# Experts' token lists built in SBUF by one-hot products, with DRAM lists only for experts over 384 tokens

## The chip, the cores and the metric

The kernel runs on one core of a Trainium2 chip. The metric is the device time of one execution in microseconds; less is better. Engines are named as in the profile: PE (TensorE matmuls) and PEld (its weight loads), DVE (VectorE), ACT (ScalarE), POOL (GpSimd) and SP (SyncE, which here only issues DMAs).

## What is computed

Block-sparse attention, and a mixture of experts with one expert for a token and a skip score, on its result. In the reference, cut to what matters:

```python
# attention: q, k, v are 4 x 8 x 768 x 64, blocks of 32, 24 blocks
mask = window | first or last block of the row or of the column | 3 sampled blocks for each query block
attn = softmax(where(mask, q @ k.T / 8, -1e9));  x = (attn @ v), as 3072 rows of 512
# experts: 8 of them, 512 -> 1024 -> 512
do_compute = x @ w_skip > 0
logits = x @ w_gate;  e = argmax(logits);  gate = softmax(logits)[e]
out = x;  out[do_compute] += gate * (relu(x @ w1[e]) @ w2[e])
```

Which tokens an expert gets is known only once attention has made `x`. So the kernel keeps, for each expert, a list of its tokens' numbers with their gates, and uses it to gather rows of `x` and to scatter the results back into `out`.

## The kernel before, in words

**Attention.** The work is a list of units: 16 dense ones (first and last query block, all keys) and then 88 sparse ones, four for each of the query blocks (tiles) 1 to 22, one for each batch. A loop over `k` (lines 645 to 704) writes out by hand what each engine gets: in step `k` come the scores `S` of unit `k + 3` (L400 in sparse units), the sums `N` of unit `k - 1`, the copy `V` and the product `A` of unit `k` (L434), the exponentials `X` of `k + 2`, the turning `T` of `k + 1` (L420) and the maxima `M` of `k + 3` (L408, L409). With the fourth unit of a tile, POOL gets the copies of the keys of the tile after next (`load_k`, L186 and L201), SP the loads of its queries and values (L208 to L220), and after `A` the stores of the finished rows to `out` (L455). In each step `fetch` (L629) adds at most two small routing steps, taken from the lists `urgent` and `todo`: their PE part behind the unit's PE work, their DVE part before or behind `M`, their POOL part at the end.

**Routing.** Tiles are routed in seven batches (`BATCHES`, L38: four of four tiles, two of three, one of two; batch 0 includes the dense tiles). `route` (L223) gives seven steps for a batch: logits on PE (`p0`, L238), their turning (`p1`, L247), three DVE steps with an exponential on ACT, the rank of each token among its expert's (`rank`, L257 to L260, which reads `cum`, the counts so far), its slot (`d3`, L280), and the address of its list entry (`d4`, L287 to L292). At the end of `d4` POOL issues one indirect DMA for each tile of the batch (L302, shown as L72, where the helper `scatter_to` stands): 128 entries of 8 bytes, token and gate, go to the DRAM tensor `lst`. All PE results of routing steps share one PSUM tile, `rps`, with a single buffer.

`lst` holds for each of 128 partitions 8 x 26 entries (`E * LC`): entry `c` of partition `p` is the token number `128 c + p` of the expert. It is first filled with "no token" by a DMA from ACT's queue (L138 to L141).

**Hand-over.** Near the end of attention `pick_first` (L510) takes the fullest expert so far as first one; `look_first` (L534) counts again, reads the first two chunks of that expert's list (`le`, L547, POOL's queue), gathers these 256 rows of `out` into `xe` (L551 to L553) and turns them for PE (`rows`, L555 to L564). The line with `timed` (L644) sets the steps of `k` at which its five parts enter `urgent`. From unit 94 on, SP loads the first weights (L488), and POOL makes the low part of the first one (L494).

In `If(pv > 1)` (L978 to L1016) the first expert's matrix product runs on these early rows while the seventh batch (tiles 21 and 22, `last`) is routed between its eight blocks: `beside` (L983) lists what goes between. Then `counts` and `lists` (L836, L847) read the token counts and the whole list back into SBUF (`lt`, through SP's queue), `order_lists` (L850) puts the first expert in front, and POOL gathers further rows (`rows`, L856). The queue of SP holds behind that read the second half of a weight (`load_w("2", 1, 1, 2)`) and the next weights. PE turns the third chunk of the first expert (L1002, shown as L588) between two parts of the second product.

**The other experts.** A loop over seven experts (L1034 to L1036) with branches on the count of tokens (`gemm1_any`, `outputs`) covers up to 384 tokens (three chunks, `CS`) of each. Whoever has more is treated behind it, in `If(top > CG * CS)` (L1040 to L1059), which is not entered with these inputs: no row of the profile has one of its lines.

Of the kernel before, what the change touches and what calls it, by code (L numbers as in the profile page):

```python
# [41 lines left out]
def tile_kernel(ctx, tc, qs, qd, kt, v, sb, wg, w1, w2, out):  # L42
# [3 lines left out]
    dram = ctx.enter_context(tc.tile_pool(name="dram", bufs=1, space=DRAM))  # L46

    lst = dram.tile([P * E * LC, 2], I32, name="lst")
# [174 lines left out]
    def route(xta, tiles):  # L223

        T = len(tiles)
        st = {}
        lgv = lambda: st["lg"][:, :, 0:E]
# [25 lines left out]
        def rank():  # L253
# [20 lines left out]
            lambda: V.tensor_copy(out=small("pay", [P, T, 2], I32, 2)[:, :, 0], in_=tokens),  # L274
# [8 lines left out]
            lambda: V.reciprocal(out=st["pay"].bitcast(F32)[:, :, 1], in_=st["es"]),  # L283
# [8 lines left out]
            lambda: V.scalar_tensor_tensor(out=small("adr", None, I32, 2), in0=st["lo"], scalar=float(E * LC), in1=st["hi"], op0=ALU.mult, op1=ALU.add),  # L292
# [95 lines left out]
    class Sparse:  # L388
# [61 lines left out]
        def after(self):  # L450
# [19 lines left out]
            if i == tiles[-1]:  # L470
                todo.extend(lambda n=n: route_step(g, tiles, n) for n in range(7))
# [61 lines left out]

    def look_first():  # L534
# [4 lines left out]
        le = rt.tile([P, 2, 2], I32, name="le")  # L539
        early["l"] = le  # L540
# [4 lines left out]
        def fetch_list():  # L545
            er = nc.gpsimd.value_load(perm[0:1, 0:1], min_val=0, max_val=E - 1)
            nc.gpsimd.dma_start(out=le, in_=lst.rearrange("(p c) w -> p c w", p=P)[:, bass.ds(er * LC, 2), :])  # L547

        def fetch_rows():
            early["x"] = [rt.tile([P, DM], F32, name="xe", bufs=2) for z in range(2)]  # L550
            for z in range(2):  # L551
                nc.gpsimd.memset(early["x"][z], 0.0)
            early["g"] = [gather(early["x"][z], le[:, z, 0:1]) for z in range(2)]  # L553
# [17 lines left out]
        ], fetch_list), (None, [], fetch_rows),  # L571
# [72 lines left out]
    timed = {nu - 22 + n: (pick_first, n) for n in range(3)} | {nu - z: (look_first, n) for n, z in enumerate((12, 11, 9, 5, 4))}  # L644
# [75 lines left out]
    lt = mc.tile([P, E * LC, 2], I32, name="lt")  # L720
    ends = mc.tile([P, CS, 2], I32, name="ends")
    lsw = mc.tile([P, LC, 2], I32, name="lsw")
# [111 lines left out]
    lst3 = lst.rearrange("(p c) w -> p c w", p=P)  # L834

# [11 lines left out]
    def lists():  # L847
        nc.sync.dma_start(out=lt, in_=lst3)

    def order_lists():  # L850
        er = nc.vector.value_load(perm[0:1, 0:1], min_val=0, max_val=E - 1)
        nc.vector.tensor_copy(out=lsw, in_=lt[:, bass.ds(er * LC, LC), :])
        nc.vector.tensor_copy(out=lt[:, bass.ds(er * LC, LC), :], in_=lt[:, 0:LC, :])
        nc.vector.tensor_copy(out=lt[:, 0:LC, :], in_=lsw)

    def rows(p, cr):  # L856
        for c in cr:
            gather(xs[p % 2][c], lt[:, p * LC + c, 0:1])
# [12 lines left out]
    def close(p, c, z, xg, m=P):  # L871
        a = p * LC + c
        finish(z, xg, ltf[:, a, 1:2], lt[:, a, 0:1], m)

    def halves(p, c, y):

        wh, wl = wview("2", p)
        cs, a = slice(P * c, P * c + P), p * LC + c
# [89 lines left out]

    wt.update({"2" + t: wp2.tile([P, 4096], F32R, name=f"w2{t}") for t in "hl"})
# [8 lines left out]
    with tc.If(pv > 1) as ahead:  # L978
        px, p0, p1, d1, d2, rank, d3, d4 = last[0]()
        le = early["l"]  # L980
# [18 lines left out]
        finish(0, early["x"][0], le.bitcast(F32)[:, 0, 1:2], le[:, 0, 0:1])  # L999
# [4 lines left out]
        finish(1, early["x"][1], le.bitcast(F32)[:, 1, 1:2], le[:, 1, 0:1])  # L1004
# [26 lines left out]
    for z in range(2):  # L1031
        nc.vector.tensor_scalar(out=ends[:, :, z], in0=lt[:, (E - 1) * LC:(E - 1) * LC + CS, 0], scalar1=2.0, scalar2=float(z), op0=ALU.mult, op1=ALU.add)
# [7 lines left out]
    with tc.If(top > CG * CS):  # L1040
        for e in range(E):
            a = e * LC
            n = tokens_of(e)
            with tc.If(n > CG * CS):
# [4 lines left out]
                with tc.For_i(CS, (n + (CG - 1)) // CG, 2) as c:  # L1049
                    cur = mp.tile([P, 2, 2], I32, name="cur", bufs=1)  # L1050
                    nc.vector.tensor_copy(out=cur, in_=lt[:, bass.ds(c + a, 2), :])
# [55 lines left out]
```

## Time and profile before

| | us |
|---|---|
| runs: 601.20, 601.09, 596.47; median | 601.09 |
| profiled execution, own time | 606.04 |
| its span | 604.3 |
| PE busy in it | 513.6 |
| POOL busy in it | 216.6 |

The profile is of one execution, whose time is 4.95 us above the median of the runs. Its span leaves out 1.7 us around it. In the answers below a row of a timeline has the start, the time and the engine, then line, operation, what it writes and reads with the shapes, and how many instructions are merged; in brackets stands how long the engine had been idle and what ended that. "issue" means that the engine waited for nothing that the profile shows. L72 is the helper of all scatters, so its tiles (`lst`, or `out`) tell which one it is.

### The profile page before, as it was taken

Reading aid. Unit: us, or ns where it says so; the run is one execution under the profiler, and the core shown is the slowest. Engines: PE = TensorE matmul, PEld = TensorE weight load, DVE = VectorE, ACT = ScalarE, POOL = GpSimd, SP = SyncE. Lnnn points to the kernel's source line nnn. Section 1 sums busy time; section 2 is a strip of 40 time slices with the busy share of each in tenths; the row PEclk is TensorE's granted clock in tenths of the full one; section 3 lists DMA queues with packets and bytes.
Section 4 is the critical chain, followed back from the end, with each engine's and each line's share of the span. In section 5 each row is a group of like instructions: output and inputs, shape, how many; then the busy total and the mean of one; then the engine's idle time right before and its main releaser. Section 6 shows DMA issues by size and latency. Waiting matters only on the chain.

```text
span 604.3 us, 16232 instructions
## 1 busy us (share of the span) xinstructions
PE 513.6 (85%) x5842; PEld 382.3 (63%) x5842; DVE 369.8 (61%) x1019; ACT 251.8 (42%) x576; POOL 216.6 (36%) x236
## 2 busy tenths in 40 slices
PE   7999999899898899996979768896887958859991
PEld 4777665466565465563668558694776946737981
DVE  4877578478577777787776066544466572735510
ACT  3444455355364355462733055343153535423500
POOL 2016363564655355646372321300404040602011
PEclk9999999799899699897988898987899888979997
DMA  9999899688799499788894415441625454630000
GB/s 295 342 299 236 190 259 243 153 219 211 174 215 232 115 227 224 167 229 214 247 322 142 172 27 179 172 180 24 218 108 178 152 189 158 214 125 26 19 33 22
DMA packets 49507, 108.03 MB, mean 179 GB/s; under 512 B 7175, under 2 KB 35208, under 8 KB 43842
## 3 DMA queue, kind: packets, MB, share of 16 engines
q1 hardware_dynamic: 43760, 84.69, 51.3%
q0 software_dynamic: 5008, 20.69, 9.7%
q8 instruction: 88, 1.44, 1.0%
q14 instruction: 73, 0.60, 0.3%
q10 hardware_dynamic: 578, 0.61, 0.3%
HBM read 96.34 MB, written 12.30 MB: 180 GB/s over the span
## 4 chain that ended last, share of the span: by engine, by line
PE 34%; issue 28%; DMA 21%; DVE 8%; POOL 3%; SPq 2%; POOLq 1%; ACT 0%; ACTq 0%; DVEq 0%
PE sp L400 11%; PE op L434 7%; PE tp L420 6%; DMA kts<-w 5%; DMA out<-o,lt 5%; DMA x<-out,lt 4%; DMA lst<-pay,adr 4%; PE op L356 4%; PE sp L321 3%; DVE m L409 3%; DVE m L408 3%; PE tp L344 2%; DMA out<-xs 2%; POOL out L72 1%; DVE xs L447 1%
## 5 line engine op out<-in xcount | busy, mean ns | idle before, releaser
L400 PE MATMUL sp<-kg,q 128*64 128x256 f32 x704 | 102.0, 408 | 2.8 <-issue 2.7
L424 ACT COPY pt<-tp 128x512 f32<-128x512 f32 x88 | 51.7, 588 | 108.1 <-PE tp L420 96.7
L408 DVE TENSOR_REDUCE m<-sp 128x2 f32<-128x512 f32 x88 | 60.2, 684 | 43.3 <-PE sp L400 35.5
L72 POOL DMA_INDIRECT out<-o,lt x17 | 19.4, 1139 | 179.2 <-DVE o L829 178.9
L201 POOL TENSOR_TENSOR kg<-kts,onesf 128x512 f32<-128x512 f32 x66 | 82.0, 1273 | 0.0
L415 ACT ACTIVATE pr<-sp,m 128x256 f32<-128x256 f32 x176 | 74.4, 478 | 8.0 <-DVE rs L445 8.0
L746 PE MATMUL hp<-xh,w1h 128*128 128x256 f32 (+3 forms) x192 | 61.3, 319 | 16.7 <-issue 8.3
L186 POOL TENSOR_SCALAR kg<-kts 128x512 f32<-128x512 f32 x50 | 30.1, 627 | 125.5 <-PE sp L400 87.4
L400 PEld LDWEIGHTS sp<-kg,q 128*64 128x64 f32 x704 | 45.2, 141 | 36.5 <-issue 24.5
L420 PE MATMUL tp<-ident,pr 128*128 128x128 f32 x352 | 61.8, 297 | 4.4 <-issue 4.4
L434 PEld LDWEIGHTS op<-va,pt 128*32 128x32 f32 x1376 | 31.9, 112 | 47.3 <-ACT pt L424 24.9
L747 PE MATMUL hp<-xl,w1h 128*128 128x256 f32 (+3 forms) x192 | 60.6, 316 | 0.0
L748 PE MATMUL hp<-xh,w1l 128*128 128x256 f32 (+3 forms) x192 | 60.5, 315 | 0.0
L751 ACT ACTIVATE hh<-hp 128x256 fp32r<-128x256 f32 (+2 forms) x56 | 21.2, 381 | 93.6 <-PE hp L748 51.6
L434 PE MATMUL op<-va,pt 128*32 128x65 f32 x1376 | 49.5, 232 | 11.3 <-DVE xs L447 8.5
L434 PE MATMUL op<-vb,pt 128*32 128x65 f32 x1376 | 50.6, 227 | 3.1 <-issue 2.9
L754 DVE SCALAR_TENSOR_TENSOR hl<-hp,hh 128x256 fp32r<-128x256 f32 (+2 forms) x56 | 23.4, 419 | 46.8 <-ACT hf L753 28.4
L746 PEld LDWEIGHTS hp<-xh,w1h 128*128 128x128 f32 x192 | 39.1, 204 | 19.1 <-issue 19.1
L420 PEld LDWEIGHTS tp<-ident,pr 128*128 128x128 f32 x352 | 38.9, 145 | 14.2 <-issue 6.9
L812 PE MATMUL yp<-w2h,hh 128*128 128x512 f32 x112 | 45.0, 402 | 2.7 <-ACT w1h L492 1.6
L813 PE MATMUL yp<-w2l,hh 128*128 128x512 f32 x112 | 44.1, 394 | 0.3 <-DVE o L829 0.3
L814 PE MATMUL yp<-w2h,hl 128*128 128x512 f32 x112 | 44.2, 394 | 0.0
(207 smaller groups left out, 1013.2 us busy)
## 6 DMA issues: line engine op xcount, KB each, us to landing
vb<-v SPq DMA_DIRECT2D x68, 260.0 KB
va<-v SPq DMA_DIRECT2D x48, 260.0 KB
kts<-w SPq DMA_DIRECT2D x6, 2048.0 KB
kts<-w POOLq DMA_DIRECT2D x6, 2048.0 KB
q<-qs SPq DMA_DIRECT2D x22, 512.0 KB
vt<-v SPq DMA_DIRECT2D x16, 390.0 KB
kts<-w SPq DMA_DIRECT2D x12, 512.0 KB
kts<-kt SPq DMA_DIRECT2D x15, 384.0 KB
```

Of the source, the lines that this page charges most:

```text
L201: nc.gpsimd.tensor_tensor(out=kg[x][:, :, c0:c0 + BS], in0=kts[:, :, bass.ds(kr * BS, BS)], in1=onesf[:, 0:BS].unsqueeze(1).broadcast_to([ ...
L400: nc.tensor.matmul(out=self.sp[64 * j:64 * j + 64, g, :], lhsT=qt[self.i][:, p, :], rhs=kg[self.x][:, p, :], start=True, stop=True)
L408: lambda: nc.vector.reduce_max(out=self.mx, in_=self.sp, axis=AX.X),
L415: nc.scalar.activation(out=self.pr[:, g, :], in_=self.sp[:, g, :], func=AF.Exp, bias=self.mx[:, g:g + 1], scale=SCALE)
L420: nc.tensor.transpose(out=self.tp[:, u, :], in_=self.pr[:, u // 2, (u % 2) * P:(u % 2) * P + P], identity=ident)
L424: nc.scalar.copy(out=self.pt, in_=self.tp)
L434: nc.tensor.matmul(out=self.op[32 * hh:32 * hh + 32, g, :], lhsT=self.pt[:, 2 * g + t, 32 * hh:32 * hh + 32], rhs=vt[:, 8 * self.b + 4 * g ...
L746: nc.tensor.matmul(out=hp[:, 0:w], lhsT=wh[:, f, k, :], rhs=xh[:, k, 0:w], start=(k == 0), stop=False)
L747: nc.tensor.matmul(out=hp[:, 0:w], lhsT=wh[:, f, k, :], rhs=xl[:, k, 0:w], start=False, stop=False)
L748: nc.tensor.matmul(out=hp[:, 0:w], lhsT=wl[:, f, k, :], rhs=xh[:, k, 0:w], start=False, stop=(k == NK1 - 1))
L812: nc.tensor.matmul(out=yp, lhsT=hh[:, f, cs], rhs=wh[:, f, :], start=(f == 0), stop=False)
L814: nc.tensor.matmul(out=yp, lhsT=hl[:, f, cs], rhs=wh[:, f, :], start=False, stop=(f == NK2 - 1))
```

## The change

The lists are kept in SBUF as floating-point numbers, `lsf`, for each of 128 partitions two words (token number minus 3072, and gate) of 8 x 3 entries. An entry is put into its place by a product: for each tile POOL makes a 128x128 matrix `lo` that has a one where the slot's low seven bits say, and two 128x24 matrices `hi` that have the token's word in the column of its expert and chunk. PE multiplies them and adds the tiles of a batch up, and DVE adds the result to `lsf`. So a batch takes nine routing steps: `d4` ends with `place` on POOL instead of the scatter, then come `put` on PE and `d5` on DVE. The sum into `cum` moves from `d4` to `d5`. Two parts of `look_first` come three, and three come two units later; `le` is copied out of `lsf` by DVE. In `beside`, `put` and then `d5`, `counts` and `lists` stand one and two places later than `counts` stood. Lists read in SBUF have a stride of three chunks instead of 26 per expert. The DRAM list is made only in the last branch, for experts over 384 tokens, from the rows, columns and words that are kept for all tiles.

```diff
-    lst = dram.tile([P * E * LC, 2], I32, name="lst")
...
-    fill = kg[0].bitcast(I32).rearrange("p a c -> p (a c)")[:, 0:2 * E * LC].rearrange("p (c w) -> p c w", w=2)
-    nc.gpsimd.memset(fill[:, :, 0], N)
-    nc.gpsimd.memset(fill[:, :, 1], 0)
-    nc.scalar.dma_start(out=lst.rearrange("(p c) w -> p c w", p=P), in_=fill)
+    posi = kg[0].bitcast(I32)[:, 0, 0:P]
+    nc.gpsimd.iota(posi, pattern=[[1, P]], base=0, channel_multiplier=0)
+    pos = const.tile([P, P], F32, name="pos")
+    nc.gpsimd.tensor_copy(out=pos, in_=posi)
+    colsi = kg[0].bitcast(I32)[:, 1, 0:E * CS].rearrange("p (e c) -> p e c", e=E)
+    nc.gpsimd.iota(colsi, pattern=[[LC, E], [1, CS]], base=0, channel_multiplier=0)
+    cols = const.tile([P, E * CS], F32, name="cols")
+    nc.gpsimd.tensor_copy(out=cols, in_=colsi.rearrange("p e c -> p (e c)"))
+    lsf = const.tile([P, 2, E * CS], F32, name="lsf")
...
+    nc.gpsimd.memset(lsf, 0.0)
...
-            lambda: V.tensor_tensor(out=cum, in0=cum, in1=st["ohs"], op=ALU.add),
...
-            lambda: V.scalar_tensor_tensor(out=small("adr", None, I32, 2), in0=st["lo"], scalar=float(E * LC), in1=st["hi"], op0=ALU.mult, op1=ALU.add),
+            lambda: V.tensor_copy(out=lof, in_=st["lo"]),
+            lambda: V.tensor_copy(out=hif, in_=st["hi"]),
...
-        def scatter():
+        def place():
+            lo = st["plo"] = rt.tile([P, T * P], F32, name="lsb").rearrange("p (t x) -> p t x", t=T)
+            hi = small("phi", [P, T, 2, E * CS])
             for t in range(T):
-                scatter_to(
-                    out=lst[:, :], out_offset=bass.IndirectOffsetOnAxis(ap=st["adr"][:, t:t + 1], axis=0),
-                    in_=st["pay"][:, t, :], in_offset=None, bounds_check=P * E * LC - 1, oob_is_err=False)
+                nc.gpsimd.tensor_scalar(out=lo[:, t], in0=pos, scalar1=lof[:, t:t + 1], scalar2=1.0, op0=ALU.is_equal, op1=ALU.mult)
+                for w in range(2):
+                    nc.gpsimd.tensor_scalar(out=hi[:, t, w], in0=cols, scalar1=hif[:, t:t + 1], scalar2=pay[:, t, w:w + 1],
+                                            op0=ALU.is_equal, op1=ALU.mult)
+        def put():
+            st["lp"] = ps_r.tile([P, 2, E * CS], F32, name="rps")
+            for t in range(T):
+                nc.tensor.matmul(out=st["lp"], lhsT=st["plo"][:, t], rhs=st["phi"][:, t], start=(t == 0), stop=(t == T - 1))
+        d5 = [
+            lambda: V.tensor_tensor(out=lsf, in0=lsf, in1=st["lp"], op=ALU.add),
+            lambda: V.tensor_tensor(out=cum, in0=cum, in1=st["ohs"], op=ALU.add),
+        ]
-        return [(p0, [], None), (p1, [], None), (None, d1, None), (None, [exp] + d2, None), (rank, [], None), (None, d3, None), (None, d4, scatter)]
+        return [(p0, [], None), (p1, [], None), (None, d1, None), (None, [exp] + d2, None), (rank, [], None), (None, d3, None), (None, d4, place),
+                (put, [], None), (None, d5, None)]
...
         def fetch_list():
-            er = nc.gpsimd.value_load(perm[0:1, 0:1], min_val=0, max_val=E - 1)
-            nc.gpsimd.dma_start(out=le, in_=lst.rearrange("(p c) w -> p c w", p=P)[:, bass.ds(er * LC, 2), :])
+            er = V.value_load(perm[0:1, 0:1], min_val=0, max_val=E - 1)
+            V.tensor_copy(out=lef, in_=lsf[:, :, bass.ds(er * CS, 2)])
...
-    timed = {...} | {nu - z: (look_first, n) for n, z in enumerate((12, 11, 9, 5, 4))}
+    timed = {...} | {nu - z: (look_first, n) for n, z in enumerate((9, 8, 7, 3, 2))}
...
     def lists():
-        nc.sync.dma_start(out=lt, in_=lst3)
+        take(lt[:, :, 0], ltf[:, :, 1], lsf)
...
-        beside = [[px], [], [p0], [p1, d1], [d2], [], [], [rank, d3], [], [d4], [], [counts, lists, lambda: load_w("2", 1, 1, 2)]]
+        beside = [[px], [], [p0], [p1, d1], [d2], [], [], [rank, d3], [], [d4], [], [], [put], [d5, counts, lists, lambda: load_w("2", 1, 1, 2)]]
```

`take` is two DVE instructions that make whole numbers of the tokens and copy the gates.

More of the change, by code (lines that the diff above doesn't have):

```diff
@@ L226, in route @@
         st = {}
+        z0 = sum(len(l) for l in BATCHES[:BATCHES.index(tiles)])
+        lof, hif, pay = rows_of[:, z0:z0 + T], cols_of[:, z0:z0 + T], pays[:, z0:z0 + T]
         lgv = lambda: st["lg"][:, :, 0:E]
@@ L273, in route @@
             lambda: V.reduce_max(out=small("pm"), in_=st["pri"], axis=AX.X),
-            lambda: V.tensor_copy(out=small("pay", [P, T, 2], I32, 2)[:, :, 0], in_=tokens),
+            lambda: V.tensor_single_scalar(out=pay[:, :, 0], in_=tokens, scalar=-float(N), op=ALU.add),
             lambda: V.tensor_tensor(out=st["pri"], in0=st["pri"], in1=bc(st["pm"]), op=ALU.is_equal),
@@ L282, in route @@
             lambda: V.tensor_tensor(out=st["sl"], in0=st["sl"], in1=st["oh"], op=ALU.mult),
-            lambda: V.reciprocal(out=st["pay"].bitcast(F32)[:, :, 1], in_=st["es"]),
+            lambda: V.reciprocal(out=pay[:, :, 1], in_=st["es"]),
             lambda: V.reduce_sum(out=small("slot"), in_=st["sl"], axis=AX.X),
@@ L470, in after @@
             if i == tiles[-1]:
-                todo.extend(lambda n=n: route_step(g, tiles, n) for n in range(7))
+                todo.extend(lambda n=n: route_step(g, tiles, n) for n in range(9))
     last = []
@@ L532, in tile_kernel, with take @@
     early = {}
+    def take(ids, gates, lists):
+        nc.vector.tensor_scalar(out=ids, in0=lists[:, 0], scalar1=N + 0.25, scalar2=0.0, op0=ALU.add, op1=ALU.add)
+        nc.vector.tensor_copy(out=gates, in_=lists[:, 1])
     def look_first():
@@ L538, in look_first @@
         key, pm = (rt.tile([1, n], F32, name=m) for m, n in (("key", E), ("pm1", 1)))
-        le = rt.tile([P, 2, 2], I32, name="le")
-        early["l"] = le
+        le = rt.tile([P, 2], I32, name="le")
+        leg = rt.tile([P, 2], F32, name="leg")
+        lef = rt.tile([P, 2, 2], F32, name="lef")
+        early["l"] = le, leg
         def pe():
@@ L552, in fetch_rows @@
                 nc.gpsimd.memset(early["x"][z], 0.0)
-            early["g"] = [gather(early["x"][z], le[:, z, 0:1]) for z in range(2)]
+            early["g"] = [gather(early["x"][z], le[:, z:z + 1]) for z in range(2)]
         def rows(c):
@@ L643, in tile_kernel @@
     nu = len(units)
-    timed = {nu - 22 + n: (pick_first, n) for n in range(3)} | {nu - z: (look_first, n) for n, z in enumerate((12, 11, 9, 5, 4))}
+    timed = {nu - 22 + n: (pick_first, n) for n in range(3)} | {nu - z: (look_first, n) for n, z in enumerate((9, 8, 7, 3, 2))}
     for k in range(-LA, nu + 1):
@@ L998, in tile_kernel @@
         rows(1, range(CS))
[L999 removed]
+        finish(0, early["x"][0], leg[:, 0:1], le[:, 0:1])
         clear()
@@ L1040, in tile_kernel @@
     with tc.If(top > CG * CS):
+        lst = dram.tile([P * E * LC, 2], I32, name="lst")
+        lst3 = lst.rearrange("(p c) w -> p c w", p=P)
+        room = hf.bitcast(I32).rearrange("p a b -> p (a b)")
+        ltx, swx = (room[:, a * 2 * LC:(a + n) * 2 * LC].rearrange("p (c w) -> p c w", w=2) for a, n in ((0, E), (E, 1)))
+        adr = room[:, (E + 1) * 2 * LC:(E + 1) * 2 * LC + NC]
+        ent = mc.tile([P, NC, 2], I32, name="ent")
+        nc.gpsimd.memset(ltx[:, :, 0], N)
+        nc.gpsimd.memset(ltx[:, :, 1], 0)
+        nc.sync.dma_start(out=lst3, in_=ltx)
+        nc.vector.scalar_tensor_tensor(out=adr, in0=rows_of, scalar=float(E * LC), in1=cols_of, op0=ALU.mult, op1=ALU.add)
+        nc.vector.tensor_single_scalar(out=ent[:, :, 0], in_=pays[:, :, 0], scalar=float(N), op=ALU.add)
+        nc.vector.tensor_copy(out=ent.bitcast(F32)[:, :, 1], in_=pays[:, :, 1])
+        for t in range(NC):
+            nc.gpsimd.indirect_dma_start(out=lst[:, :], out_offset=bass.IndirectOffsetOnAxis(ap=adr[:, t:t + 1], axis=0), in_=ent[:, t, :],
+                                         in_offset=None, bounds_check=P * E * LC - 1, oob_is_err=False)
+        nc.sync.dma_start(out=ltx, in_=lst3)
+        order_lists(ltx, swx, LC)
         for e in range(E):
```

37 lines of the change are left out of this document (20 added, 17 removed).

## The prediction, made before the changed kernel was run

> **What bounds the kernel now.** I read the page first, then the matmuls of L400 (the scores, eight for each unit of sparse attention) in stretches of the attention stage, then the timeline of each engine in one stretch.
>
> ```profile
> span 604.3 us, 16232 instructions
> PE 513.6 (85%) x5842; PEld 382.3 (63%) x5842; DVE 369.8 (61%) x1019; ACT 251.8 (42%) x576; POOL 216.6 (36%) x236
> ```
>
> TensorE is the busiest, so what counts is where it stands still. Columns below: stretch, its length, PE busy with L400 (count), PEld busy (count), granted clock, DMA share, GB/s.
>
> ```profile
> 81.00:104.20 23.20, 9.38 (x72) 4.14 (x68) 1.00 1.04 264
> 104.20:119.20 15.00, 5.58 (x32) 2.42 (x32) 0.77 0.76 185
> 119.20:147.90 28.70, 13.01 (x96) 5.82 (x96) 1.00 0.82 198
> 147.90:161.50 13.60, 5.67 (x32) 2.52 (x32) 0.87 0.88 214
> 161.50:189.70 28.20, 13.01 (x96) 5.82 (x96) 1.00 0.84 202
> 189.70:207.30 17.60, 6.12 (x32) 2.51 (x32) 0.71 0.63 165
> 207.30:237.80 30.50, 14.09 (x104) 6.30 (x104) 1.00 0.87 210
> 237.80:249.20 11.40, 4.30 (x24) 1.95 (x24) 0.85 0.83 193
> 249.20:270.40 21.20, 9.76 (x72) 4.37 (x72) 1.00 0.81 201
> 270.40:288.30 17.90, 5.21 (x32) 2.23 (x32) 0.81 0.79 211
> 288.30:298.70 10.40, 4.34 (x32) 1.94 (x32) 1.00 0.94 252
> ```
>
> Six stretches run at 142.2 us for 472 matmuls, 59 units: 2.41 us a unit, at full clock. The five between take 75.5 us for 152 matmuls, 19 units, at a lower clock. At 2.41 they would take 45.8, so **29.7 us** are lost there. Each of the five begins where the list scatter of a batch runs on POOL. The fourth one:
>
> ```profile
> 237.48 1.01 POOL L72 DMA_INDIRECT lst<-pay,adr  x1 [2.67 <-DVE adr L292]
> ...
> 242.36 1.22 POOL L186 TENSOR_SCALAR kg<-kts 128x512 f32<-128x512 f32 x2
> 243.53 3.72 POOL L201 TENSOR_TENSOR kg<-kts,onesf 128x512 f32<-128x512 f32 x3
> ```
>
> ```profile
> 237.28 0.66 PE L420 MATMUL tp<-ident,pr 128*128 128x128 f32 x4
> 237.86 1.08 PE L400 MATMUL sp<-kg,q 128*64 128x256 f32 x8
> ...
> 239.69 0.33 PE L420 MATMUL tp<-ident,pr 128*128 128x128 f32 x1
> 240.34 0.31 PE L420 MATMUL tp<-ident,pr 128*128 128x128 f32 x1 [0.31 <-issue]
> 241.07 0.31 PE L420 MATMUL tp<-ident,pr 128*128 128x128 f32 x1 [0.43 <-issue]
> 241.81 0.27 PE L420 MATMUL tp<-ident,pr 128*128 128x128 f32 x1 [0.43 <-issue]
> 243.31 0.44 PE L400 MATMUL sp<-kg,q 128*64 128x256 f32 x2 [0.87 <-issue]
> ```
>
> Four transposes take 0.58 us before the scatter (237.28 to the next work at 237.86). During it they come 0.7 us apart, "issue": PE waits for no engine. From 239.69 to 243.31 it does about 0.7 us of work, so some 2.9 us go; over five batches about 15 us. The other 15 come behind it: the next tile's keys (L186, L201, 4.9 us of POOL compute) start late and shut VectorE out.
>
> ```profile
> 196.85 4.61 DVE L409 TENSOR_SCALAR m<-m 128x2 f32<-128x2 f32 x1
> ...
> 253.42 0.49 DVE L409 TENSOR_SCALAR m<-m 128x2 f32<-128x2 f32 x1
> ...
> 273.74 6.41 DVE L409 TENSOR_SCALAR m<-m 128x2 f32<-128x2 f32 x1
> ```
>
> The middle row is a quiet tile: the little L409 gets in between two POOL instructions. After scatters (first and last row) it stayed out for a whole run of them.
>
> **The change, part by part.** *Removed in attention*: 19 scatters in the five stretches (the other five lie behind the last scores), with their small DRAM writes, so I take back all 29.7 us and charge what replaces them.
>
> ```profile
> L119 POOL TENSOR_SCALAR_AFFINE_SELECT uppf<-onesf 128x128 f32<-128x128 f32 x1 | 0.3, 294 | 0.1
> L129 POOL TENSOR_SCALAR prio<-iif 128x8 f32<-128x8 f32 x1 | 0.2, 198 | 0.1
> ```
>
> *POOL adds* per tile one 128x128 compare and two of 128x24. No such compare is in the trace; by these rows 0.29 + 2 x 0.20 = 0.69 us a tile, 2.8 a batch of four, against 4.9 from first scatter to L186. But it is compute, which can shut L409 out, and L409 arrives early in it. If it slips between instructions, it loses 0.3 us as in the row of 0.49; if it waits out the batch, 2.8; if the batch joins the key copies without a pause, 2.8 + 4.9 = 7.7. I take 2.8, because the compares wait for nothing between them, of which a pipeline with scores three units ahead hides about 0.9: **1.9**.
>
> [...]
>
> *PE adds* T matmuls of 48 columns with 128x128 weights, at most the 0.58 us of four transposes with as large weights, and no less than 0.3 if they cost half; I take 0.6. They wait for the last compare: emitted one unit (2.2 us) after it started and 2.8 long, so **0.5** more; queued behind on PE are the next scores. *VectorE adds* two copies and one 128x48 add, less one address: some 0.4 us, hidden where VectorE waits for scores; without that cover up to 0.4 a batch, in the range. Sum: 1.9 + 0.6 + 0.5 = **3.0** per stretch, 15.0 for five; bounds 0.3 + 0.3 + 0.5 = 1.1 and 7.7.
>
> *At the start* two fills and one DMA go, four small constants come; POOL then sits idle, so nothing:
>
> ```profile
> 42.46 2.97 POOL L186 TENSOR_SCALAR kg<-kts 128x512 f32<-128x512 f32 x5 [38.04 <-DMA out<-xd]
> ```
>
> *The hand-over to the experts.* The early look moves two or three units later, and its two row turnings now stand as PE's last work before the first expert, then the sixth put; all three use the one routing bank.
>
> ```profile
> 304.94 0.32 PE L434 MATMUL sp<-va,pt 128*32 128x65 f32 x8
> ...
> 307.03 0.55 PE L746 MATMUL hp<-xeh,w1h 128*128 128x256 f32 x1
> ...
> 317.65 0.18 PE L257 MATMUL rps<-oh,upp 128*128 128x16 bf16 x1 [1.78 <-DVE oh L276]
> ```
>
> ```profile
> 298.91 0.59 ACT L563 CAST xeh<-rps 128x512 fp32r<-128x512 f32 x1
> ```
>
> ```profile
> L564 DVE TENSOR_TENSOR xel<-rps,xeh 128x512 fp32r<-128x512 f32 x2 | 1.4, 680 | 0.0
> ```
>
> One round is a turning (0.58), the cast (0.59), the subtraction (0.68) and three hand-overs of 0.1: 2.1 us. Starting at about 305.5, behind L434, two rounds end at 309.7. The routing step that the sixth place needs now runs after the first subtraction (307.6) and takes some 0.8, so three tiles of compares end at 308.4 + 2.1 = 310.5, and put and the first expert matmul come at about 311 instead of 307.03: **+4.0**. Then:
>
> ```profile
> 313.50 3.23 DVE L266 TENSOR_SCALAR on<-lg 128x2 f32<-128x2 f32 x1
> ```
>
> ```profile
> 313.84 2.87 POOL L973 MEMSET x<- 128x512 f32 x6
> ```
>
> ```profile
> 325.15 0.36 SPq L848 DMA_DIRECT2D lt<-lst  x1
> 326.37 2.78 SPq L488 DMA_DIRECT2D kts<-w  x2
> ```
>
> ```profile
> 339.16 0.98 PE L588 MATMUL tp<-ident,x 128*128 128x128 f32 x4 [4.14 <-DMA x<-out,lt]
> ```
>
> ```profile
> 339.20:342.50 3.30, 3.30 (x11) 2.72 (x11) 0.69 (x1) 0.59 (x1) 0.00 (x0) 0.52 0.03 10
> ```
>
> L266 is shut out by POOL's clearing of the row tiles (L973); of its 3.2 us PE felt the 1.78 in L257's row. With PE and VectorE 4 us later and POOL less so, the clearing is over by then: -1.8. Against it the seventh put can wait for its two tiles' compares, at most 2 x 0.69 = 1.4, and the count, now behind the sum, about as long for VectorE; I take 2.4 for both: **+0.6** in all. The list's reading back leaves SP's queue, where the second half of a weight (the first of the two L488 loads) stood behind it and met the row gathers. Now it can go as soon as SP reaches it, and PE arrives later: I take the whole wait of L588 back, **-4.1**, and most of the slow clock after it (3.3 us at 0.52 would be 1.7 at full clock), **-1.2**. Together 4.0 + 0.6 - 4.1 - 1.2 = -0.7; bounds -5 (no late start) and +6, where the early rows, fetched three units later and behind the stores of one more tile on SP's queue, land late and hold PE, with POOL's weight splits queued behind that fetch.
>
> **Sum** on the profiled execution: -29.7 + 15.0 - 0.7 = -15.4, so 606.04 becomes 590.6. It stands 4.95 above the runs' median of 601.09, so the runs should give **585.7**. At most those 4.95 can be gaps that only profiling makes.
>
> **Rivals.** *One instruction at a time* (chance 0.18): L409 slips in everywhere, 1.1 per stretch: -29.7 + 5.5 - 0.7 = -24.9, 576.2. The 0.49 row is for it, the 4.61 against. *Late early rows* (0.14): the upper bound of the hand-over, -29.7 + 15.0 + 6 = -8.7, 592.4. For it speaks the DMA share of 0.94 in the last stretch; against it that four units of 2.41 us lie between fetch and use. *The gaps are not the scatter's* (0.13): another thing in the same step, such as the tile loads on SP, starves PE, and the 15 us stay: -15.4 + 15 = -0.4, 600.7. Against it: quiet tiles issue the same loads without a gap; for it: the scatters behind 307 us leave PE's matmuls unbroken. [...] *POOL compute locks VectorE out* (0.08): compares and key copies join in every batch, 7.7 each: -29.7 + 38.5 - 0.7 = +8.1, 609.2. It decides from 6.1 per stretch; for it the row of 6.41, against it that key copies wait for scores issued after the compares began.
>
> **How the numbers follow.** The forecast has 0.47. A measurement here tells about 1% (6 us) from no change. Below 595.1: the forecast but for 0.02, the first rival, 0.11 of the second, 0.02 of the third: 0.76. Above 607.1: the last rival and 0.02 of the third: 0.10. Between: 0.14. The range 575 to 601 leaves out the last rival, half of the third and the far end of the first: 0.19; the forecast's own range is 580 to 592.
>
> **What would show it.** In the changed profile: sparse units near 2.41 us throughout, with no run of "issue" gaps of 0.4 in L420 or L434; L409 longest near 3 us, within the compares; the compares 0.7 us a tile; PE's first L746 some 4 us later behind the last scores, and no wait for x before L588. Wrong, if gaps stay at the same steps, or if L409 waits 5 us and more.

## The result: slower by 2.5%

The changed kernel takes 616.87 us (median of four runs, 615.63 to 620.41), the kernel before 601.14 on the same chip: a ratio of 1.0254, with a 95% interval of 1.0203 to 1.0306. The forecast was 585.7, the range ended at 601. The profiled execution took 615.63 us against 606.04.

The page after, its span and its first section:

```profile
span 614.0 us, 16366 instructions
PE 521.8 (85%) x5890; PEld 389.8 (63%) x5890; DVE 381.1 (62%) x1038; ACT 252.6 (41%) x576; POOL 230.0 (37%) x286
```

PE is busy 8.2 us longer than before and idle 1.5 us longer. The table of stretches of the scores (now L424; columns as in the prediction) tells where:

```profile
104.60:119.85 15.25, 5.22 (x32) 2.22 (x32) 0.89 0.69 178
119.85:149.30 29.45, 13.65 (x96) 6.00 (x96) 1.00 0.79 196
149.30:164.65 15.35, 5.23 (x32) 2.22 (x32) 0.89 0.70 184
164.65:193.70 29.05, 13.01 (x96) 5.82 (x96) 1.00 0.81 196
193.70:209.40 15.70, 6.12 (x32) 2.51 (x32) 0.78 0.70 185
209.40:237.60 28.20, 13.01 (x96) 5.82 (x96) 1.00 0.86 204
237.60:253.20 15.60, 5.23 (x32) 2.23 (x32) 0.89 0.70 182
253.20:274.40 21.20, 9.76 (x72) 4.37 (x72) 1.00 0.77 183
274.40:286.00 11.60, 3.88 (x24) 1.74 (x24) 0.85 0.99 259
```

The slow stretches are still there, at the same places, now with the compares in them instead of the scatters: 73.5 us for 19 units, against 75.5 before. At the 2.41 us of a quiet unit they lose 27.7 us. Not all of this is standing: PE is busy for 57.8 of the 75.5 us before and 57.9 of the 73.5 now, where 19 quiet units keep it busy for 44.7. The granted clock is lower in these stretches (0.71 to 0.87 before, 0.78 to 0.89 now) and the same matmuls take longer there (eight of L424 1.97 us at 112.69 us, 1.08 in a quiet unit); now the matmuls of the sum are in it too. The "issue" gaps have gone, and something as large has come in. The first stretch, seen on three engines:

```profile
106.09 0.73 POOL L314 TENSOR_SCALAR lsb<-pos,rows_of 128x128 f32<-128x128 f32 x1 [3.41 <-ACT pr L439]
106.83 0.85 POOL L316 TENSOR_SCALAR phi<-cols,cols_of,pays 128x24 f32<-128x24 f32 x2
...
112.26 1.20 POOL L193 TENSOR_SCALAR kg<-kts 128x512 f32<-128x512 f32 x2
113.43 3.70 POOL L208 TENSOR_TENSOR kg<-kts,onesf 128x512 f32<-128x512 f32 x3
```

```profile
110.81 0.42 PE L322 MATMUL rps<-phi,lsb 128*128 128x48 f32 x2 [0.78 <-POOL phi L316]
112.34 0.42 PE L322 MATMUL rps<-phi,lsb 128*128 128x48 f32 x2 [1.11 <-POOL phi L316]
```

```profile
106.61 0.23 DVE L433 TENSOR_SCALAR m<-m 128x2 f32<-128x2 f32 x1
108.73 0.17 DVE L433 TENSOR_SCALAR m<-m 128x2 f32<-128x2 f32 x1
112.92 4.23 DVE L326 TENSOR_TENSOR cum<-cum,ohs 128x8 bf16<-128x8 bf16 x1
```

Four tiles of compares last from 106.09 to 112.26: 1.54 us a tile, where 0.69 was reckoned. PE's sum waits for them. And L326, an add of 8 numbers a partition, takes 4.23 us: it is shut out (held back by POOL's work) until the last key copy (L208) has ended. During the compares themselves VectorE was not held: L433 took 0.17 and 0.23 us.

The second loss lies between attention and the experts. The last scores start at 300.3 us (before: 299.4), the first expert matmul at 318.21 (before: 307.03):

```profile
301.76 1.26 POOL L609 DMA_INDIRECT xe<-out,le  x1 [6.54 <-DVE m L433]
304.36 6.15 POOL L518 TENSOR_TENSOR w1l<-kts,w1h 128x512 fp32r<-128x512 f32 x5
```

```profile
308.05 1.09 PE L592 MATMUL rps<-ident,xe 128*128 128x128 f32 x4 [2.79 <-DMA xe<-out,le]
312.09 1.12 PE L592 MATMUL rps<-ident,xe 128*128 128x128 f32 x4 [1.93 <-DVE xel L595]
314.70 0.64 PE L322 MATMUL rps<-phi,lsb 128*128 128x48 f32 x2 [1.49 <-DVE xel L595]
...
318.21 0.57 PE L779 MATMUL hp<-xeh,w1h 128*128 128x256 f32 x1
```

POOL stands idle for 6.54 us before it can fetch the early rows; PE then waits 2.79 us for them. The weight splits (L518) had queued up behind it and run in one piece, and while they do, a routing step of VectorE is shut out:

```profile
305.62 4.92 DVE L290 TENSOR_SCALAR es<-es 128x3 f32<-128x3 f32 x1
```

So place and sum of the sixth batch come late too. The seventh batch's sum then makes PE wait 2.84 and 1.08 us within the first expert, and the next expert starts at 373.96 us instead of 361.87. The later stage gives 2.4 of these 12.1 back: 9.7 us of span.

### The profile page after: what moved, and what is told of

Same layout as the page of the kernel before. It is cut to its first block, busy times and chain, and to the rows that moved or that the text cites. A ratio compares the mean times of both kernels' runs of the same rounds, so it can differ in the third digit from the quotient of the medians.

```text
span 614.0 us, 16366 instructions
## 1 busy us (share of the span) xinstructions
PE 521.8 (85%) x5890; PEld 389.8 (63%) x5890; DVE 381.1 (62%) x1038; ACT 252.6 (41%) x576; POOL 230.0 (37%) x286
## 5 line engine op out<-in xcount | busy, mean ns | idle before, releaser
L424 PE MATMUL sp<-kg,q 128*64 128x256 f32 x704 | 101.5, 408 | 1.1 <-issue 1.1
L208 POOL TENSOR_TENSOR kg<-kts,onesf 128x512 f32<-128x512 f32 x66 | 82.0, 1271 | 0.0
L432 DVE TENSOR_REDUCE m<-sp 128x2 f32<-128x512 f32 x88 | 60.1, 684 | 28.1 <-PE sp L424 26.8
L193 POOL TENSOR_SCALAR kg<-kts 128x512 f32<-128x512 f32 x50 | 30.0, 620 | 124.6 <-PE sp L424 87.6
L424 PEld LDWEIGHTS sp<-kg,q 128*64 128x64 f32 x704 | 44.6, 141 | 32.8 <-issue 20.5
L787 DVE SCALAR_TENSOR_TENSOR hl<-hp,hh 128x256 fp32r<-128x256 f32 (+2 forms) x56 | 23.5, 420 | 57.9 <-ACT hf L786 26.7
L444 PE MATMUL tp<-ident,pr 128*128 128x128 f32 x352 | 58.6, 290 | 0.0
L458 PE MATMUL op<-vb,pt 128*32 128x65 f32 x1376 | 48.4, 226 | 0.8 <-issue 0.8
L847 PE MATMUL yp<-w2h,hl 128*128 128x512 f32 x112 | 44.7, 399 | 0.0
```

Of the source, the lines that this page charges most:

```text
L208: nc.gpsimd.tensor_tensor(out=kg[x][:, :, c0:c0 + BS], in0=kts[:, :, bass.ds(kr * BS, BS)], in1=onesf[:, 0:BS].unsqueeze(1).broadcast_to([ ...
L424: nc.tensor.matmul(out=self.sp[64 * j:64 * j + 64, g, :], lhsT=qt[self.i][:, p, :], rhs=kg[self.x][:, p, :], start=True, stop=True)
L432: lambda: nc.vector.reduce_max(out=self.mx, in_=self.sp, axis=AX.X),
L444: nc.tensor.transpose(out=self.tp[:, u, :], in_=self.pr[:, u // 2, (u % 2) * P:(u % 2) * P + P], identity=ident)
L458: nc.tensor.matmul(out=self.op[32 * hh:32 * hh + 32, g, :], lhsT=self.pt[:, 2 * g + t, 32 * hh:32 * hh + 32], rhs=vt[:, 8 * self.b + 4 * g ...
L847: nc.tensor.matmul(out=yp, lhsT=hl[:, f, cs], rhs=wh[:, f, :], start=False, stop=(f == NK2 - 1))
```

## The experiments

"Scores" is the time from the first to the last matmul of a sparse unit's scores, "hand-over" from there to the first expert matmul; both are differences of starts in the profiled execution, rounded to 0.1 us. "Time" is the median of the runs. The kernels ran on several chips, where the kernel before takes 596.7 to 601.1 us; each ratio is to the kernel before on the same chip. Where no time stands, lists stay empty, there is one run, and only the first two columns count. The time without a ratio is too scattered to compare.

| kernel | scores | hand-over | time | ratio to before, 95% |
|---|---|---|---|---|
| before | 242.7 | 7.6 | 601.1 | |
| after | 242.9 | 17.9 | 616.9 | 1.0254 (1.0203 to 1.0306) |
| after, early look one or two steps earlier | 241.4 | 13.8 | 609.4 | 1.015 (1.005 to 1.0249) |
| after, no compares, no sum | 215.5 | 13.0 | | |
| before, no scatters | 218.6 | 7.9 | | |
| before, scatters that write nothing | 235.7 | 7.6 | | |
| after, compares on VectorE | 223.0 | 18.8 | 594.0 | 0.9889 (0.9823 to 0.9954) |
| after, sum two steps later | 237.1 | 18.8 | 613.0 | 1.0225 (1.0145 to 1.0305) |
| after, compares but no sum | 240.5 | 14.3 | | |
| after, sum but no compares | 217.8 | 17.6 | | |
| after, compares behind the key copies | 238.3 | | 617.4 | 1.0332 (1.0218 to 1.0446) |
| sum two steps later, scaling on ScalarE | 221.0 | 22.2 | 597.1 | 0.9982 (0.9941 to 1.0023) |
| before, scaling on ScalarE | 222.0 | 8.2 | 582.6 | 0.9748 (0.9644 to 0.9853) |
| after, compares on VectorE and early look | 225.0 | 14.5 | 589.9 | 0.9859 (0.9768 to 0.995) |
| before, scaling as a product of two tiles | 231.8 | 7.9 | 596.6 | |
| after, scaling on ScalarE | 243.1 | 18.3 | 612.7 | 1.0258 (1.0198 to 1.0317) |
| all that helped | 220.7 | 8.0 | 583.3 | 0.9737 (0.9686 to 0.9788) |

### The fetch of the early rows

```diff
-    timed = {...} | {nu - z: (look_first, n) for n, z in enumerate((9, 8, 7, 3, 2))}
+    timed = {...} | {nu - z: (look_first, n) for n, z in enumerate((10, 9, 8, 5, 4))}
```

> The changed kernel with the early look put back by one to three units, as far as the sum allows: count, list, fetch of the early rows ahead of the stores of tile 20, turnings in their old units. Theory (the hand-over is lost because the early rows are fetched late, behind the stores of one more tile): the first expert matmul (L779) comes at about 312 us instead of 318.2, and the whole run takes 610, about 7 less than the changed kernel. Rival (the hand-over is lost to the place, the sum and their POOL work in front of the first expert, whenever the rows come): the first expert matmul stays within 2 us of 318.2 and the run takes 615 to 617.

The first expert matmul came at 311.49 us, the run took 609.4, 7.5 less than the changed kernel. The theory's numbers held: 6.7 of the 11.2 us by which the first expert came late, and the time with them, hang on one or two steps of the loop. (Later texts call these the old steps; only the two turnings are back at theirs, the other three parts still stand one or two steps later than in the kernel before.)

```profile
286.07 1.26 POOL L609 DMA_INDIRECT xe<-out,le  x1 [5.93 <-DVE rs L469]
```

```profile
311.49 0.55 PE L779 MATMUL hp<-xeh,w1h 128*128 128x256 f32 x1 [0.26 <-PE rps L322]
```

The fetch goes 15.7 us earlier than in the changed kernel (301.76), and what holds the first expert now is the sum of the sixth batch.

### What attention would take without either way of making lists

```diff
-        return [..., (None, d4, place), (put, [], None), (None, d5, None)]
+        return [..., (None, d4, None), (None, [], None), (None, d5, None)]   # d5 without the add into lsf
```

> The changed kernel without the compares on POOL and without the matmuls and the sum of the lists: the lists stay empty, so no row is gathered and none written back by the experts; only the time up to the first expert matmul is to be read. Theory (the compares eat what the scatters gave back): the five stretches run at the 2.4 us a unit of the quiet ones, the last scores end at about 272 us instead of 299.6, and the first expert matmul comes about 30 us earlier, at 286 to 290. Rival (something else in the same steps is slow): the last scores end at 290 or later.

```diff
-        return [..., (None, d3, None), (None, d4, scatter)]
+        return [..., (None, d3, None), (None, d4, None)]
```

> The kernel before without its 24 list scatters: the lists stay at no token, so no row is gathered and none written back by the experts; only the time up to the first expert matmul is to be read. Theory (the gaps are the scatter's): no run of issue gaps in L420, all stretches at 2.4 us a unit, the last scores end at about 269 us instead of 298.7. Rival (the gaps are those of another thing in the same step, such as the tile loads): the gaps stay and the last scores end at 284 or later.

The scores take 215.5 and 218.6 us. So in attention the scatters did cost some 24 us (242.7 less 218.6) and the compares with the sum cost 27.4 (242.9 less 215.5). The change replaced one by the other.

### Is it the writing of the entries?

```diff
-            lambda: V.tensor_scalar(out=small("off"), in0=st["on"], scalar1=-NEVER, scalar2=NEVER, op0=ALU.mult, op1=ALU.add),
+            lambda: V.tensor_scalar(out=small("off"), in0=st["on"], scalar1=0.0, scalar2=NEVER, op0=ALU.mult, op1=ALU.add),
```

> The kernel before with the 24 scatters issued as before, but every address out of bounds, so that none of them writes to DRAM (lists at no token, nothing gathered later; only the time up to the first expert matmul is to be read). Theory (the small DRAM writes take the gaps' 15 us, POOL's own time for the scatters delays the key copies and takes the other 15): the issue gaps go, the last scores end at about 284 us. [...] Rival two (all is the writes): 269 to 272.

Neither the theory nor a rival: 235.7 us, and most of the gaps stay. What PE's L420 waited on "issue" (us, times) in the kernel before, without scatters, and with scatters that write nothing:

```profile
  issue: 11.3, 25
```

```profile
  issue: 0.2, 1
```

```profile
  issue: 8.2, 21
```

The scatter is needed for the gaps, its writes to DRAM are not. (The profile counts as many packets on POOL's DMA queue as in the kernel before, 5008, so the requests were still made.)

### Compares, sum, or what stands behind them?

```diff
-            for t in range(T):
-                nc.gpsimd.tensor_scalar(out=lo[:, t], ...)          # and two for hi
+            nc.vector.tensor_tensor(out=lo, in0=x, in1=lof.unsqueeze(2).broadcast_to([P, T, P]), op=ALU.is_equal)
+            nc.vector.tensor_tensor(out=eq, in0=y, in1=hif.unsqueeze(2).broadcast_to([P, T, E * CS]), op=ALU.is_equal)
+            nc.vector.tensor_tensor(out=hi, in0=eq ..., in1=pay ..., op=ALU.mult)
```

> The changed kernel with the compares of a batch on VectorE as three broadcast operations (rows 128x512, columns 128x96, columns times token and gate 128x192) in place of the three per tile on POOL. Theory (POOL's 1.54 us a tile is what attention loses: PE waits on it in the sum and the key copies start late behind it): some 1.2 us a batch on VectorE, the last scores at 280 to 284 us instead of 300.3, the run at about 597. Rival (the matmuls of the sum and the two routing steps more are the loss, whoever compares): the last scores at 295 or later, the run at 611 or more.

```diff
-        return [..., (None, d4, place), (put, [], None), (None, d5, None)]
+        return [..., (None, d4, place), (None, [], None), (None, [], None), (put, [], None), (None, d5, None)]   # cum in d4
```

> The changed kernel with two empty routing steps between the compares and the sum of the lists, the running counts taken in the step of the addresses as in the kernel before. Theory A (PE's 15.6 us of waits for the compares are a loss of their own): the sum waits no more, the last scores end at about 288 us instead of 300.3, the run takes 606. Theory B (the key copies behind the compares on POOL are late anyway, so the wait only moves to the next scores and their consumers): the last scores at 296 to 300, the run at 613 to 617.

```diff
-                (put, [], None), (None, d5, None)]
+                (None, [], None), (None, d5, None)]   # d5 without the add into lsf
```

> The changed kernel with the compares on POOL but without the matmuls and the add that sum them into the lists (lists stay empty, nothing gathered by the experts; only the time up to the first expert matmul is to be read). The kernel without both ended its last scores at 274.8 us, the changed one at 300.3. Theory A (PE's wait is the loss): 284 to 288. Theory B (late key copies and VectorE shut out are the loss): 295 or later.

```diff
-                nc.tensor.matmul(out=st["lp"], lhsT=st["plo"][:, t], rhs=st["phi"][:, t], ...)
+                nc.tensor.matmul(out=st["lp"], lhsT=pos, rhs=cols2, ...)   # place left out
```

> The changed kernel without the compares, but with as many matmuls of the same shapes on constants and an add of the same size into a tile nobody reads (lists stay empty, nothing gathered; only the time up to the first expert matmul is to be read). If PE's own work for the sum is 0.3 to 0.6 us a batch, as it was costed, the last scores end at 276 to 278 us against 274.8 without both; rival (a matmul between the scores costs more than its duration): 282 or later.

The sum alone costs 2.3 us of scores (217.8 less 215.5), 0.46 a batch, near the 0.6 of the prediction. The compares alone, with nobody waiting for their result, cost 25.0 (240.5 less 215.5), 5.0 a batch. Putting the sum later takes PE's wait for them from 15.6 us to 7.6 in all, in attention from 10.2 to nothing, and gains 5.8 of scores. So PE's wait is not the main part: it stands in part where time is lost anyway. On VectorE the three operations take 0.68, 0.25 and 0.36 us a batch, and the scores take 223.0 us: 594.0, 23 us less than on POOL.

Why compares that nobody waits for cost 5 us a batch is seen in the run without the sum. Its POOL, VectorE and PE at the first stretch:

```profile
107.85 0.73 POOL L314 TENSOR_SCALAR lsb<-pos,rows_of 128x128 f32<-128x128 f32 x1 [7.56 <-DVE cols_of L301]
...
114.01 1.20 POOL L193 TENSOR_SCALAR kg<-kts 128x512 f32<-128x512 f32 x2
115.18 3.69 POOL L208 TENSOR_TENSOR kg<-kts,onesf 128x512 f32<-128x512 f32 x3
122.53 1.20 POOL L193 TENSOR_SCALAR kg<-kts 128x512 f32<-128x512 f32 x2 [3.66 <-PE sp L423]
```

```profile
115.08 3.82 DVE L432 TENSOR_SCALAR m<-m 128x2 f32<-128x2 f32 x1
123.27 0.48 DVE L432 TENSOR_SCALAR m<-m 128x2 f32<-128x2 f32 x1
```

```profile
119.63 0.32 PE L457 MATMUL op<-va,pt 128*32 128x65 f32 x8 [3.20 <-DVE xs L470]
```

In a quiet tile (122.53, last POOL row) the key copies begin the moment PE releases their buffer, and L432 (the scaling of the maxima) gets in between the one-input copies L193 and the two-input copies L208: 0.48 us. Behind compares the copies begin when POOL is free, without a pause. L432 then asks at 115.08, 0.1 us before the first L208 starts, and is let in at 118.9, when the third has ended. Everything behind it on VectorE is late, and PE stands 3.20 us.

### Two tests of the shut-out

If that is so, compares that don't delay the key copies should cost nothing, and a kernel without L432 on VectorE should not lose the time.

```diff
+        if BATCHES.index(tiles) <= 3:
+            return head + [(None, d4, None), (None, [], place)] + 4 * [(None, [], None)] + [(put, [], None), (None, d5, None)]
```

> The changed kernel with the compares of the first four batches one routing step later, so that they stand on POOL behind the next tile's key copies and not ahead of them, and the sum four steps further; the other three batches as they were. Theory K (the compares cost nothing themselves: they push the key copies into a phase in which a small VectorE instruction asks while the three two-input copies run, and is shut out until the last of them ends, 3.5 to 4.6 us a batch in every run with compares on POOL): no VectorE instruction over 2 us in the four stretches, the last scores at about 282 us instead of 300.3, the run at about 600. Rival C (compares on POOL cost their time wherever they stand): the last scores at 295 or later, the run at 611 or more.

```diff
-                lambda: nc.vector.tensor_single_scalar(out=self.mx, in_=self.mx, scalar=-SCALE, op=ALU.mult),
+                lambda: nc.scalar.mul(out=self.mx, in_=self.mx, mul=-SCALE),
```

> The kernel with the sum two steps later (613 us, last scores at 293.5, L433 shut out for 3.6 to 4.6 us in each of five stretches), and the scaling of the row maxima in L433 moved from VectorE to ScalarE for the sparse units. Theory K: what was shut out is no longer on VectorE, so the last scores come at 277 to 281 us and the run takes about 599. Rival (the key copies' own lateness holds the scores, or another VectorE instruction is shut out in its place): the last scores at 289 or later, the run at 609 or more.

The first missed: 238.3 us of scores, the last ones at 295.3, as rival C had it. Its rows say why. The compares now end just as the *next* tile's copies are due, these follow without a pause again, and the same instruction (here L435) is shut out again:

```profile
119.45 0.87 POOL L316 TENSOR_SCALAR phi<-cols,cols_of,pays 128x24 f32<-128x24 f32 x2
120.28 1.21 POOL L193 TENSOR_SCALAR kg<-kts 128x512 f32<-128x512 f32 x2
121.45 3.71 POOL L208 TENSOR_TENSOR kg<-kts,onesf 128x512 f32<-128x512 f32 x3
```

```profile
121.45 3.73 DVE L435 TENSOR_SCALAR m<-m 128x2 f32<-128x2 f32 x1
```

The moment of asking is not what decides. L435 asks here just as the first L208 starts, and so does the same instruction (there L434) in the run with the compares on VectorE, where POOL had stood idle before the copies; it is let in when the first L208 ends:

```profile
110.80 1.20 POOL L193 TENSOR_SCALAR kg<-kts 128x512 f32<-128x512 f32 x2 [5.31 <-PE sp L425]
111.97 3.74 POOL L208 TENSOR_TENSOR kg<-kts,onesf 128x512 f32<-128x512 f32 x3
```

```profile
111.97 1.28 DVE L434 TENSOR_SCALAR m<-m 128x2 f32<-128x2 f32 x1
```

What the long waits have in common is that the key copies follow other work of POOL, compares or scatters, without a pause. In the sparse stage of all kept traces 48 scalings, sums and products of SBUF tiles asked during such copies, and 44 waited until the third L208 (L201 in the kernel before) had ended; 526 asked during copies that began after a pause, and none took more than 1.52 us. No run changed the pause alone.

So the shut-out behind the compares stands, but a batch of 6.2 us and copies of 4.9 don't fit into a tile's ten without touching each other; "cost nothing themselves" was too much. (No matmul of its first expert reads the early rows: it took the other branch, so its total isn't comparable.) The second held: 221.0 us of scores instead of 237.1, 597.1 us instead of 613.0, by one 128x2 instruction moved to another engine. What is left above the kernel without compares and sum is 5.5 us (221.0 less 215.5), so the lateness of the copies by itself costs little.

### Which instruction, and which form

```diff
-                lambda: nc.vector.tensor_single_scalar(out=self.mx, in_=self.mx, scalar=-SCALE, op=ALU.mult),
+                lambda: nc.scalar.mul(out=self.mx, in_=self.mx, mul=-SCALE),   # in the kernel before
```

> The kernel before with the same scaling moved to ScalarE for the sparse units. If half of the 29.7 us that its scatter stretches lose is VectorE shut out behind key copies, as the prediction had it (rows of 4.61 and 6.41 us, and three of 1.2 to 1.7), that half goes in part: the last scores at 286 to 292 us instead of 299.4, the run at 588 to 593. Rival (the issue gaps are the loss and the shut-out is hidden behind them): the last scores at 296 to 300, the run at 597 to 602.

This went far beyond the expectation: 222.0 us of scores, 582.6 us. All scatters are there, 1.28 us apart, and PE runs through them without a gap:

```profile
226.09 0.97 POOL L72 DMA_INDIRECT lst<-pay,adr  x1 [0.30 <-issue]
227.37 0.98 POOL L72 DMA_INDIRECT lst<-pay,adr  x1 [0.31 <-issue]
```

```profile
226.78 0.66 PE L420 MATMUL tp<-ident,pr 128*128 128x128 f32 x4
```

So the gaps needed two things, a scatter on POOL and L409 on VectorE. Is it VectorE, or the form of L409?

```diff
-                lambda: nc.vector.tensor_single_scalar(out=self.mx, in_=self.mx, scalar=-SCALE, op=ALU.mult),
+                lambda: nc.vector.tensor_tensor(out=self.mx, in0=self.mx, in1=msc, op=ALU.mult),   # msc: a constant tile
```

> The kernel before with the scaling of the row maxima kept on VectorE, but as a product of two tiles (maxima times a constant tile) in place of the product with an immediate. Moved to ScalarE it took 582.6 us and lost the issue gaps and the shut-outs together. Theory F (it is the form with one SBUF input and an immediate that clashes with POOL, both with the scatters and with the key copies): as on ScalarE, last scores at 280 to 284 us, 583 to 587. Theory R (any VectorE operation that reads only SBUF is shut out by the key copies, since they read SBUF too, while the scatters mind only the immediate form): no issue gaps, but L411 still waits 4 us behind key copies in some stretches, last scores at 286 to 293, 588 to 594. Rival (only getting it off VectorE helps): 597 to 602 with gaps.

Theory R, in the trace: 231.8 us of scores, L422's gaps gone, but the new form shut out behind the key copies in all five stretches, 2.9 to 4.2 us. (Its ten runs lie between 585.7 and 600.8 us, too wide to tell more.)

```profile
  issue: 0.7, 4
```

```profile
153.38 4.19 DVE L411 TENSOR_TENSOR m<-m,msc 128x2 f32<-128x2 f32 x1
```

And in the changed kernel, where L326 was the one shut out, with only L433 moved:

```diff
-                lambda: nc.vector.tensor_single_scalar(out=self.mx, in_=self.mx, scalar=-SCALE, op=ALU.mult),
+                lambda: nc.scalar.mul(out=self.mx, in_=self.mx, mul=-SCALE),   # in the changed kernel
```

> The changed kernel with only the scaling of L433 moved to ScalarE. In the changed kernel the instruction shut out for 4 us in each stretch is the add of the counts (L326), not L433. Theory (whichever VectorE instruction that reads only SBUF asks first behind the compares is shut out until the key copies end): L326 still waits about 4 us, the last scores come at 296 to 300 us, the run takes 611 to 617. Rival (L433 is the one that matters): 598 to 604, as with the later sum.

612.7 us and 243.1 of scores, the last ones at 302.6 (a little beyond the 296 to 300): nothing gained, as the theory said. Whichever scaling, sum or product of SBUF tiles asked first was held (L432 3.82 us, L435 3.73, L411 4.19, L326 4.23). "Any instruction that reads only SBUF" is too wide: the reciprocal L470 (L446 in the kernel before) reads only SBUF and took 0.17 us wherever it fell.

```profile
163.30 4.23 DVE L326 TENSOR_TENSOR cum<-cum,ohs 128x8 bf16<-128x8 bf16 x1
```

### What the change is worth once both are avoided

```diff
-                nc.gpsimd.tensor_scalar(out=lo[:, t], ...)
+            nc.vector.tensor_tensor(out=lo, ...)   # and two for hi, as above
-    timed = {...} | {... enumerate((9, 8, 7, 3, 2))}
+    timed = {...} | {... enumerate((10, 9, 8, 5, 4))}
```

> The changed kernel with the compares on VectorE and the early look put back to its old steps, both together. Alone the first took 594.0 us, with its first expert matmul 18 us behind the last scores (the kernel before: 8), the second took 7 off the changed kernel. If the two add up: 587, first expert matmul at about 294 us. Rival (with POOL free the early fetch is no longer late): 592 to 594.

589.9 us, between the two, with the first expert matmul at 299.4 us instead of 294. Here PE stands 6.88 us in front of the last sum, because the cast that `place` needs is shut out by POOL's weight splits and by its clearing of the row tiles (L1006):

```profile
289.07 4.97 POOL L519 TENSOR_TENSOR w1l<-kts,w1h 128x512 fp32r<-128x512 f32 x4 [1.57 <-ACT w1h L517]
293.98 2.85 POOL L1006 MEMSET x<- 128x512 f32 x6
```

```profile
292.88 3.98 DVE L300 CAST rows_of<-lo 128x3 f32<-128x3 int32 x1
```

```profile
298.08 1.48 PE L323 MATMUL rps<-phi,lsb 128*128 128x48 f32 x6 [6.88 <-DVE rs L470]
```

The last kernel adds the scaling of the maxima on ScalarE and takes that sum behind the first block of the first expert:

```diff
-        beside = [[px], [], [p0], [p1, d1], ...]
+        beside = [[px], [tail[0]], [tail[1], p0], [p1, d1], ...]   # tail: put and d5 of the sixth batch
```

> The changed kernel with what the runs point to, together: compares on VectorE, early look at its old steps, scaling of the row maxima on ScalarE, and the last sum of the attention loop moved behind the first block of the first expert, so that PE doesn't wait for it (its wait was 6.9 us where the compares were on VectorE). From 589.9 us of the first two alone: the scaling should give 5 (one shut-out of 1.1 to 1.9 us in each stretch), the moved sum 5 to 7, so 578 to 580, below the kernel before with the scaling moved (582.6). Rival (the sum's wait only moves into the first expert): 584 to 586.

583.3 us, 2.6% below the kernel before, hand-over 8.0, but short of the 578 to 580: the first expert starts 11.5 us earlier than in the run before it, the next expert only 8.0, so part of the wait moved into the first expert, as the rival had it. It is faster than both kernels. But the kernel before with its 24 scatters, and one instruction moved, takes 582.6 (ratio 0.9748 against 0.9737 here). No run shows a gain of lists without DRAM beyond that.

## Why the prediction was wrong, point by point

- **Where the time was lost before**: right. 29.7 us in the five stretches were read off; without scatters 24 of them go.
- **What takes it**: half right. "Issue" gaps and shut-outs are both there. But the gaps are neither the scatter's alone, as the sum had it, nor another thing's, as the third rival had it: they come of the scatter together with L409, and either one taken away ends them (11.3 to 0.2 us). Nor do they come with packets of the instruction queues: in the kernel before none moves from 151.6 to 155.5 us, where PE has three of these gaps and still goes on.
- **"0.69 us a tile"**: too small by a factor of 2.2. Rows of compute with immediates (294 and 198 ns) priced compares whose scalars are columns of SBUF: 745 and 459 ns.

```profile
L316 POOL TENSOR_SCALAR phi<-cols,cols_of,pays 128x24 f32<-128x24 f32 x48 | 21.5, 459 | 0.0
L314 POOL TENSOR_SCALAR lsb<-pos,rows_of 128x128 f32<-128x128 f32 x24 | 17.9, 745 | 23.9 <-DVE cols_of L301 10.0 <-PE hp L780 8.3 <-ACT pr L439 3.4
```

  The batch of four took 6.2 us, more than the four scatters' 4.9 to 5.0, so behind it the key copies started later, not earlier. This is the first step that failed: "2.8 a batch" against "4.9 from first scatter to L186".
- **Residual "3.0 per stretch"**: 5.5 (27.4 over five). The sum's 0.6 was right (0.46). The 1.9 of L409 was put at the compares, which hold next to nothing; it is the copies behind them that do, with 4 us. The fourth rival came nearest, a stop of compares and copies in one, and its condition, that the batch joins the key copies without a pause, is the one that the traces bear out; it had 8 chances in 100 and was to decide from 6.1 us a stretch.
- **Hand-over "-0.7"**: the second step that failed, by about as much: +11.2 to the start of the next expert (12.1, less the 0.9 of attention). "+4.0" for the first expert matmul was 10.3. The runs split it: 4.1 go with the earlier steps of the early look (17.9 to 13.8); most of the rest goes with the sixth sum no longer standing before the first expert (14.5 to 8.0 in the last two kernels, where the scaling was moved too). The bound of +6 named the mechanism, rows landing late with the weight splits queued behind (that the stores hold the fetch is not shown: for POOL's 6.54 us the profile names a scaling on VectorE), but not what the splits then do to VectorE (4.92 us). The 4.14 us of waiting for row tiles did go, as predicted (first row below, no wait); batch seven's sum and count took them back (2.84, 1.08 and 1.12 us of PE's waits).

```profile
353.13 0.66 PE L621 MATMUL tp<-ident,x 128*128 128x128 f32 x4
```

```profile
334.23 0.45 PE L322 MATMUL rps<-phi,lsb 128*128 128x48 f32 x2 [2.84 <-POOL phi L316]
```

- **Sum**: attention +0.9 instead of -14.7, hand-over +11.2 instead of -0.7, the stage behind -2.4: +9.7 of span.

## What to carry to other kernels

Price a new operation from a row with the same operand kinds, and ask of work put on a free engine what stands behind it in that engine's queue: here the key copies, joined to it without a pause, shut VectorE out for four microseconds. When a stretch is slow beside two engines' work, move the smallest instruction first; a 128x2 scaling on another engine was worth as much (2.5%) as the removal of all scatters was meant to bring. A step that an early look, a fetch or a queue depends on is part of the change, even where only its number moves.

## What the runs showed of the hardware

- Scalings, sums and products of SBUF tiles on VectorE (L409, L433, L326, L411) that asked while POOL copied keys waited, in 44 of 48 cases, until the third two-input copy had ended where the copies followed other work of POOL without a pause (3.7 to 4.2 us for those that asked up to 0.5 us before the first of them or at its start). Where POOL had stood idle before the copies, they were let in when one copy ended (1.28 us for L434 at 111.97 us in the run with the compares on VectorE, and 0.41 for L435 at 112.51 us in the run with the compares behind the copies). The pause is not the whole rule: the cast L300 was held for 3.98 us by splits that began after 1.57 us of idling and by the clearing behind them. Two kinds were not held within such copies, in the kernel before with the scaling on ScalarE: the reduction L408 at 230.76 us, which reads PSUM (0.69 us), and the reciprocal L446 at 231.55 us, which reads SBUF (0.17 us). Both forms of the scaling were held behind key copies, L409 for 4.61 us and L411 for 4.19. The hold outlasted one POOL instruction (3.7 us for L435 against the 1.24 of one copy), and POOL's compares delayed L433 by no more than 0.06 us in the first stretch (0.17 and 0.23).
- Scatters on POOL and a 128x2 product with an immediate on VectorE made PE issue one instruction in 0.7 us for 2 to 4 us (L420 at 239.69, 240.34, 241.07 and 241.81 us in the kernel before). The gaps in front of L420 went from 11.3 us to 0.7 with the other form, and to 0.2 with the product on ScalarE or without the scatters; in the fourth stretch POOL's scatters start 1.28 to 1.32 us apart whether the product is on VectorE or on ScalarE. So the gaps depend on work of two other engines; by which way the stop reaches PE no run here shows.
